# A spectral filter gated by a ReGLU network on one core: the second pair of row tiles turned by a transposing DMA in place of TensorE

## The chip, the cores and the metric

The kernel runs on one core of a Trainium2 chip. The metric is the device time of one execution in microseconds (us), median of three runs.

## The reference

```python
def reference(A_x, A_w_r, A_w_i, B_x, B_W_gate, B_W_up, B_W_down):
    def _A_ref(x, w_r, w_i):
        X = jnp.fft.rfft2(x, axes=(-2, -1)) * (w_r + 1j * w_i)
        return jnp.fft.irfft2(X, s=(S, D), axes=(-2, -1))
    def _B_ref(x, W_gate, W_up, W_down):
        gate = jnp.einsum("bsd,df->bsf", x, W_gate)
        up = jnp.einsum("bsd,df->bsf", x, W_up)
        h = gate * (gate > 0) * up
        return jnp.einsum("bsf,fd->bsd", h, W_down)
    x = A_x
    xn = _layernorm(x, axis=-1)
    return x + _A_ref(xn, A_w_r, A_w_i) * _silu(_B_ref(xn, B_W_gate, B_W_up, B_W_down))
```

`x` is 1 x 2048 x 512, the filter 2048 x 257 (real and imaginary part), the gate and up weights 512 x 1376, the down weights 1376 x 512, all in 32 bits.

## The kernel before

**Tiles.** The 2048 rows are 16 row tiles of 128 (partitions) by 512. They are handled in pairs, `c` = 0 to 7, and two pairs make a block of four row tiles, on which the gate and up products work. So pairs 0 and 1, row tiles one to four, are block 0; its transposed input is `xT0`, with columns 0 and 1 from pair 0 and 2 and 3 from pair 1. The 11 column blocks of the gate and up weights (10 of 128, the last of 96) come in groups `[0], [1], [2], [3,4], [5,6], [7,8], [9,10]`; `raw<g>_0` is the gate part of group g as loaded (32 bits), `raw<g>_1` the up part, and `wgu<g>` its 16-bit form.

**Products in three.** Every large product is made of 16-bit matmuls. A factor is split into a 16-bit high part and a low part (the rounding error, again in 16 bits), and the three passes high x high, high x low and low x high are added up in PSUM. A gate or up product is named `gu<block>_<column block>_<0 gate, 1 up>`; for one of them four slices of the 512 times three passes make a dozen matmuls, in the order of the slices: weights high with input high, weights high with input low, weights low with input high (`product`, L858). So the third matmul of a dozen needs the weights' low half, and the second the input's.

**Scaling the weights.** Before the split a group is multiplied by a power of two. ACT squares the raw weights and sums along the row (`squares`, L609); TensorE sums over the partitions with a column of ones (the `small<-m,ones` and `sum<-m,ones` matmuls); DVE makes the power of two from it (`csc`, three short steps, in some groups a fourth, `ups`; `group_scale`, L623); then the high half is written by ACT or DVE (`wgu<-raw,csc`) and the low half by DVE (SCALAR_TENSOR_TENSOR `wgu<-raw,csc,wgu`; `group_split`, L641).

**The start.** Row tiles are loaded by SP's queue, normalised (`stats`, `deviation`, `normalise`, L363 to L422: DVE statistics, ACT's square root, DVE's scaling to `xf<c>`), and turned, since a matmul takes the 512 along the partitions. Pair 0 is turned on TensorE in 32 bits, and its gate and up products with groups 0 and 1 run as fp32 matmuls straight from the raw weights (`gu<-xTf,raw`), so that TensorE has work while the weights are scaled. Pair 1 is turned on TensorE as well (`turn_row`, L496: eight fp32 transposes into PSUM, tile `head1`; then a cast for the high half and a subtraction for the low half, both out of PSUM). Pairs 2 to 7 go another way (`turn`, L438): ACT copies `xf<c>` to 16 bits (`x16_<c>`, high half), DVE or POOL subtracts for the low half, and SP issues one transposing DMA into `xT`, for pairs below 4 straight from SBUF (`DIRECT`, L61).

From there the A path (the two-dimensional transform as matmuls, stages y, xx, z, v, s) and the B path (gate, up, rectified product, down) are interleaved on TensorE.

**What sets the order.** Nothing is scheduled on the chip: each engine works its own list of instructions in order, with semaphores between engines, and SP issues nearly all DMAs, likewise in order. The lists come from a plan (`Plan`, L186). The code describes steps with what they read and write (`step`, L206); `run` (L233) emits them by the table `ORDER`; `PLACE` gives for each step that has a choice (`either`, L225) the engine, D for DVE, P for POOL, A for ACT; `SLOTS` gives the buffer of each tile. `folds` (`fold`, L530) make the even and odd parts of a pair's rows for the A path (`eo`, `ee`, `xs`).

Where the choice for pair 1 stands:

```python
if TURN1 == "PE":                       # L1291
    turn_row(1, 0)
    turn_row(1, 1)
...
            if k > 1 or k and TURN1 == "SP":     # L1300
                turn(k, LOWS[k])
```

Of the kernel before, what the change touches and what calls it, by code (L numbers as in the profile page):

```python
# [43 lines left out]
NORM, TURN1 = (('DVE', 'DVE'), ('DVE', 'DVE')), 'PE'  # L44
# [24 lines left out]
    4, 5, 6, 7, 8, 9, 10, 11, 12, 13, 14, 15, 16, 17, 32, 34, 33, 35, 36, 38, 37, 40, 39, 41, 143, 18, 19, 20, 21, 22, 23, 24, 25, 26, 27, 28, 51, 50,  # L69
    29, 30, 31, 144, 53, 42, 68, 52, 56, 57, 145, 146, 60, 61, 43, 45, 44, 46, 90, 89, 54, 147, 69, 92, 47, 48, 55, 480, 481, 91, 482, 483, 49, 70,  # L70
    79, 64, 99, 71, 93, 94, 100, 484, 58, 65, 97, 455, 62, 137, 120, 490, 140, 141, 138, 486, 487, 80, 66, 63, 485, 142, 139, 59, 492, 67, 119, 72,
    110, 73, 74, 95, 102, 101, 1235, 488, 489, 96, 109, 103, 410, 82, 77, 75, 98, 516, 104, 491, 493, 81, 107, 159, 76, 83, 105, 518, 456, 106, 122,
    149, 78, 112, 496, 124, 121, 123, 125, 528, 126, 408, 517, 148, 108, 175, 129, 494, 111, 113, 114, 150, 176, 177, 519, 529, 115, 178, 510, 182, 0,
    530, 497, 465, 151, 152, 522, 409, 629, 116, 131, 133, 511, 179, 628, 183, 117, 84, 407, 135, 136, 495, 626, 184, 185, 627, 413, 180, 181, 645,
    130, 118, 186, 520, 411, 127, 644, 132, 412, 414, 187, 512, 128, 134, 523, 1581, 87, 630, 466, 153, 154, 156, 467, 155, 631, 531, 158, 188, 524,
    189, 85, 161, 191, 415, 416, 554, 86, 192, 193, 219, 190, 632, 642, 220, 217, 525, 417, 157, 499, 513, 88, 546, 218, 160, 643, 633, 638, 162, 163,
    221, 498, 500, 418, 419, 420, 165, 1205, 526, 194, 501, 521, 552, 196, 646, 421, 197, 504, 195, 547, 164, 647, 422, 423, 222, 548, 502, 424, 648,
    534, 198, 505, 425, 634, 532, 649, 635, 166, 234, 426, 427, 553, 650, 654, 469, 167, 549, 640, 555, 223, 506, 507, 636, 508, 527, 453, 540, 428,
    651, 793, 168, 199, 536, 541, 791, 429, 225, 514, 430, 454, 431, 652, 224, 639, 584, 515, 255, 230, 271, 535, 252, 432, 612, 597, 231, 655, 433,
    556, 611, 503, 585, 434, 509, 637, 226, 542, 1, 656, 435, 436, 641, 598, 599, 610, 272, 537, 273, 437, 438, 256, 274, 227, 571, 572, 439, 600,  # L80
# [12 lines left out]
    780, 833, 354, 396, 339, 340, 767, 398, 399, 400, 470, 804, 805, 806, 834, 835, 836, 784, 787, 807, 808, 809, 810, 783, 785, 250, 355, 356, 837,
    786, 799, 800, 1171, 811, 801, 812, 464, 294, 357, 358, 359, 361, 341, 342, 324, 344, 477, 295, 343, 297, 296, 360, 402, 299, 298, 300, 328, 362,
    301, 401, 404, 363, 346, 1172, 302, 303, 788, 349, 403, 364, 304, 366, 838, 365, 368, 1206, 406, 802, 813, 306, 305, 839, 840, 814, 817, 843, 570,
    377, 367, 345, 369, 370, 1173, 347, 815, 307, 308, 841, 845, 844, 310, 847, 848, 846, 818, 348, 378, 381, 471, 472, 309, 850, 851, 380, 379, 382,
    385, 849, 386, 852, 1207, 854, 853, 857, 405, 1204, 473, 474, 855, 862, 1234, 864, 856, 860, 863, 350, 1169, 861, 865, 866, 867, 475, 858, 859,
    1208, 1209, 387, 869, 1174, 373, 374, 1210, 1238, 1239, 371, 372, 868, 383, 1240, 870, 871, 872, 1184, 803, 873, 1175, 1176, 1211, 876, 1177, 874,
    1178, 1212, 1213, 1236, 1237, 879, 1214, 875, 880, 881, 883, 1216, 1577, 1215, 1217, 882, 1179, 1181, 885, 1218, 1219, 1221, 884, 583, 886, 1220,
    888, 1180, 819, 1185, 1223, 889, 1186, 1222, 1182, 1241, 1187, 1224, 1225, 890, 891, 892, 893, 877, 1183, 887, 1226, 820, 1188, 1227, 1245, 902,  # L100
    904, 894, 1565, 1189, 903, 1242, 375, 895, 1190, 821, 351, 905, 1228, 1191, 1193, 1243, 1192, 1194, 376, 1246, 1244, 906, 909, 1229, 1230, 898,
    1195, 822, 907, 910, 1248, 896, 1231, 897, 1196, 913, 1247, 1249, 1250, 352, 1197, 823, 1232, 908, 911, 914, 923, 1198, 1199, 1200, 824, 825, 899,
    1233, 912, 826, 827, 1252, 915, 917, 816, 1561, 1253, 924, 878, 925, 1251, 927, 928, 1264, 1265, 1268, 1201, 1266, 1254, 918, 926, 930, 931, 1269,
    1270, 1202, 1255, 1256, 1203, 916, 828, 948, 900, 1267, 609, 1257, 1295, 934, 1275, 1276, 932, 933, 1258, 1271, 929, 1272, 919, 1277, 1274, 1273,
# [1360 lines left out]
```

## Time and profile before

| | |
|---|---|
| median of 3 runs | 388.42 us (387.67 to 388.53) |
| the profiled execution | 388.55 us |
| its span, first to last instruction | 386.8 us |
| mean granted TensorE clock | 1.000 |
| TensorE matmuls | 378.9 us busy, 98% of the span |
| VectorE (DVE) | 307.8 us, 80% |
| ScalarE (ACT) | 252.0 us, 65% |
| GpSimd (POOL) | 85.3 us, 22% |
| bytes moved by DMA | 77.95 MB, mean 202 GB/s |

In the profile PE is TensorE's matmuls, PEld its weight loads, which run beside matmuls, and SPq the DMAs issued by SP. All recorded instructions carry one line (L169, a helper), so they are told apart by the names of their tiles: `out<-in`, with the number of a block or group left out. An instruction row gives its start in us, its length, the engine, the instruction with tiles and shape, how many stand in the row, and in brackets the idle time before it with what ended it. Where several follow one another without a gap, the distance from start to start is less than the length, since an instruction's end overlaps the next one's beginning.

### The profile page before, as it was taken

Reading aid. Unit: us, or ns where it says so; the run is one execution under the profiler, and the core shown is the slowest. Engines: PE = TensorE matmul, PEld = TensorE weight load, DVE = VectorE, ACT = ScalarE, POOL = GpSimd, SP = SyncE. Lnnn points to the kernel's source line nnn. Section 1 sums busy time; section 2 is a strip of 40 time slices with the busy share of each in tenths; the row PEclk is TensorE's granted clock in tenths of the full one; section 3 lists DMA queues with packets and bytes.
Section 4 is the critical chain, followed back from the end, with each engine's and each line's share of the span. In section 5 each row is a group of like instructions: output and inputs, shape, how many; then the busy total and the mean of one; then the engine's idle time right before and its main releaser. Section 6 shows DMA issues by size and latency. Waiting matters only on the chain.

```text
span 386.8 us, 8906 instructions
## 1 busy us (share of the span) xinstructions
PE 378.9 (98%) x3525; PEld 261.3 (68%) x3525; DVE 307.8 (80%) x557; ACT 252.0 (65%) x490; POOL 85.3 (22%) x79
## 2 busy tenths in 40 slices
PE   8899999999999999999999999999999999999995
PEld 6755545445778777646888877755587787877544
DVE  6899999999678997994669882559377874399996
ACT  4899998999985565645476554764647662476411
POOL 2200203000232303001422087051105020214330
PEclk9999999999999999999999999999999999999999
DMA  7989878897579659878645647553652054999997
GB/s 259 407 288 305 245 134 255 274 259 199 186 188 289 191 174 289 272 146 236 198 158 185 146 114 217 164 143 90 205 130 78 2 162 117 232 212 248 223 254 188
DMA packets 67834, 77.95 MB, mean 202 GB/s; under 512 B 29073, under 2 KB 40945, under 8 KB 67793
## 3 DMA queue, kind: packets, MB, share of 16 engines
q1 hardware_dynamic: 66352, 74.77, 66.7%
q0 software_dynamic: 1440, 2.62, 4.3%
q8 instruction: 27, 0.44, 0.5%
q14 instruction: 15, 0.11, 0.1%
HBM read 46.95 MB, written 26.76 MB: 191 GB/s over the span
## 4 chain that ended last, share of the span: by engine, by line
PE 93%; DMA 2%; DVE 2%; ACT 1%; issue 0%; POOL 0%; SPq 0%; ACTq 0%
PE dn L169 28%; PE gu L169 17%; PE sb L169 15%; PE sa L169 10%; PE sc L169 10%; PE s L169 3%; PE z L169 3%; PE xx L169 3%; PE y L169 2%; DMA raw<-in_wu 2%; PE v L169 2%; DMA x<-in_x 1%; DVE t L169 1%; ACT wgu L169 1%; DVE xt L169 1%; DVE sv L169 0%
## 5 line engine op out<-in xcount | busy, mean ns | idle before, releaser
L169 PE MATMUL dn<-wds,h 128*128 128x512 f16 (+2 forms) x528 | 118.9, 372 | 0.0
L169 PEld LDWEIGHTS <-wgu 128*128 128x128 f16 x960 | 92.6, 98 | 37.7 <-issue 2.2
L169 PEld LDWEIGHTS <-h 128*128 128x128 f16 (+1 forms) x594 | 54.3, 98 | 51.4 <-issue 2.1
L169 PEld LDWEIGHTS <-wT 128*128 128x128 f16 x540 | 52.4, 98 | 9.3 <-issue 0.6
L169 PE MATMUL gu<-xT,wgu 128*128 128x512 f16 (+1 forms) x240 | 47.8, 358 | 0.0
L169 PE MATMUL sa<-xT,wgu 128*128 128x256 f16 x360 | 44.2, 273 | 0.0
L169 PE MATMUL sb<-xS,wT 128*128 128x256 f16 x360 | 44.2, 273 | 0.0
L169 PE MATMUL sc<-xS,wgu 128*128 128x256 f16 x180 | 22.1, 273 | 0.0
L169 PE MATMUL sc<-xT,wT 128*128 128x256 f16 x180 | 22.1, 273 | 0.0
L169 PE MATMUL sb<-xS,wgu 128*128 128x256 f16 x180 | 22.1, 273 | 0.0
L169 DVE TENSOR_TENSOR sc<-sb,sk 128x512 f32<-128x512 f32 x15 | 10.5, 698 | 12.7 <-PE sb L169 11.5
L169 ACT ACTIVATE sb<-sa 128x512 f32<-128x512 f32 x15 | 8.8, 585 | 13.7 <-PE sa L169 13.2
L169 DVE TENSOR_TENSOR t<-v,t 128x1024 f16<-128x1024 f32 x8 | 9.8, 1222 | 9.5 <-ACT t L169 9.4
L169 DVE TENSOR_TENSOR sr<-sb,sr 128x512 f32<-128x512 f32 x15 | 10.3, 686 | 8.6 <-PE sb L169 5.4
L169 PE MATMUL gu<-xT,wgt 128*64 128x256 f16 (+1 forms) x144 | 17.0, 309 | 0.0
L169 ACT ACTIVATE sq<-sc 128x512 f32<-128x512 f32 x15 | 8.9, 594 | 11.3 <-PE sc L169 7.9
L169 POOL TENSOR_TENSOR x<-xf,x 128x512 f16<-128x512 f32 x5 | 5.6, 1118 | 48.1 <-PE sb L169 38.8
L169 ACT ACTIVATE g<-dn,cdi 128x512 f32<-128x512 f32 (+1 forms) x16 | 10.5, 672 | 7.6 <-PE dn L169 7.5
L169 ACT ACTIVATE h<-se 128x512 f16<-128x512 f32 x15 | 9.4, 627 | 8.7 <-DVE se L169 6.0
L169 DVE TENSOR_TENSOR z<-z,z 128x1024 f16<-128x1024 f32 x8 | 9.8, 1223 | 6.6 <-ACT z L169 6.6
L169 ACT ACTIVATE t<-v 128x1024 f16<-128x1024 f32 x8 | 8.2, 1023 | 10.0 <-PE v L169 9.9
L169 ACT ACTIVATE p<-pf 128x1024 f16<-128x1024 f32 x8 | 8.5, 1057 | 9.4 <-DVE pf L169 7.7
(217 smaller groups left out, 740.8 us busy)
## 6 DMA issues: line engine op xcount, KB each, us to landing
rw<-in_wl SPq DMA_DIRECT2D x8, 512.0 KB, 4.2
A_d<-t SPq DMA_DIRECT2D x16, 256.0 KB, 3.7
wt<-in_wl SPq DMA_DIRECT2D x8, 512.0 KB, 4.3
at<-A_d SPq DMA_DIRECT2D x8, 512.0 KB, 4.6
C_d<-t SPq DMA_DIRECT2D x16, 256.0 KB, 3.2
ct<-C_d SPq DMA_DIRECT2D x16, 256.0 KB, 5.6
xf<-in_x SPq DMA_DIRECT2D x6, 512.0 KB, 5.0
N_d<-xf SPq DMA_DIRECT2D x6, 512.0 KB, 3.5
```

What stands on the lines that cost most here:

```text
L169: return lambda *args, **kw: self.tc.keep_in_program_order(f(*args, **kw))
```

## The change

Pair 1 (row tiles three and four) is turned as pairs 2 and 3 are. The eight fp32 transposes on TensorE, the two casts and the two subtractions from PSUM are gone. In their place ACT makes two copies to 16 bits, DVE two subtractions, and SP one transposing DMA of 128 x 16 x 128 from `x16_1` in SBUF to columns 2 and 3 of `xT0`. The three tables that set order, engines and buffers are new as a whole; the code is otherwise the same.

```diff
-NORM, TURN1 = (('DVE', 'DVE'), ('DVE', 'DVE')), 'PE'
+NORM, TURN1 = (("DVE", "DVE"), ("DVE", "DVE")), "SP"
...
 ORDER = (
-    4, 5, 6, 7, 8, 9, 10, 11, 12, 13, 14, 15, 16, 17, 32, 34, 33, 35, 36, 38, 37, 40, 39, 41, 143, 18, 19, 20, 21, 22, 23, 24, 25, 26, 27, 28, 51, 50,
...
+    4, 5, 6, 32, 34, 7, 8, 9, 10, 11, 12, 13, 33, 35, 14, 15, 16, 17, 18, 36, 19, 20, 21, 22, 23, 24, 25, 26, 27, 38, 37, 40, 467, 28, 39, 42, 29, 51,
```

The numbers behind a tile's name in the rows below are those of its buffer and version; `x4` counts instructions of one form.

TensorE, from the first fp32 products (`gu<-xTf,raw`) to the first 16-bit product of pair 1 (`gu0_0_0<-xT0,wgu0`). Before:

```order
MATMUL small_149<-m0_204,ones_127 128x2
MATMUL gu0_0_0_255<-xTf0_216,raw0_0_197 128x128 x4
MATMUL gu0_0_0_255<-xTf1_226,raw0_0_197 128x128 x4
MATMUL gu0_0_1_265<-xTf0_216,raw0_1_195 128x128 x4
MATMUL gu0_0_1_265<-xTf1_226,raw0_1_195 128x128 x4
LDWEIGHTS ones_127
MATMUL sum3_284<-m3_246,ones_127 128x2
MATMUL gu0_1_291<-xTf0_216,raw1_0_208 128x128 x4
MATMUL head1_303<-unit_101,xf1_249 128x128 x8
MATMUL gu0_1_291<-xTf0_216,raw1_1_275 128x128 x4
MATMUL gu0_1_291<-xTf1_226,raw1_1_275 128x128 x4
MATMUL gu0_1_291<-xTf1_226,raw1_0_208 128x128 x4
```

The same place in the changed kernel:

```order
MATMUL gu0_0_1_258<-xTf0_230,raw0_1_197 128x128 x4
LDWEIGHTS ones_127
MATMUL small_149<-m0_199,ones_127 128x2
MATMUL gu0_1_270<-xTf0_230,raw1_1_255 128x128 x4
MATMUL gu0_0_1_258<-xTf1_237,raw0_1_197 128x128 x4
LDWEIGHTS ones_127
MATMUL small_149<-m1_242,ones_127 128x2
LDWEIGHTS ones_127
MATMUL sum3_299<-m3_287,ones_127 128x2
MATMUL gu0_1_270<-xTf1_237,raw1_1_255 128x128 x4
MATMUL gu0_1_270<-xTf0_230,raw1_0_224 128x128 x4
MATMUL sum4_333<-m4_294,ones_127 128x2
```

The transposes `head1` are gone, the sums of groups 0 and 1 (`small`) come between the fp32 products, and the sum of group 4 (`sum4`), which came later before, stands ahead of the last of them.

VectorE, before, from the scaling of group 3's up weights to the low half of group 3's gate (`wgu3_105<-raw3_0`), which the third matmul of `gu0_4_0`, the gate dozen of column block 4, reads:

```order
TENSOR_SCALAR wgu3_105<-raw3_1_238,csc_122 128x1024
CAST xT0_296<-head1_303 128x512 x2
TENSOR_TENSOR xT0_296<-head1_303,xT0_296 128x512 x2
SCALAR_TENSOR_TENSOR h32_0_0_337<-gu0_0_1_265,ups_134,r0_0_310 128x256
SCALAR_TENSOR_TENSOR wgu0_102<-raw0_1_195,csc_122,wgu0_102 128x512
TENSOR_SCALAR csc_122<-small_149 128x2
TENSOR_SCALAR csc_122<-csc_122 128x2 x2
TENSOR_SCALAR ups_134<-csc_122 128x1
SCALAR_TENSOR_TENSOR wgu3_105<-raw3_0_240,csc_122,wgu3_105 128x1024
```

The same place in the changed kernel, after the two subtractions into `x16_1` and the `csc` steps and folds behind them:

```order
SCALAR_TENSOR_TENSOR wgu1_103<-raw1_0_224,csc_122,wgu1_103 128x512
TENSOR_TENSOR ee0_313<-eo0_227 128x4x129
TENSOR_SCALAR wgu0_102<-raw0_0_201,csc_122 128x512
TENSOR_SCALAR csc_122<-sum4_333 128x2x2
TENSOR_SCALAR csc_122<-csc_122 128x2x2 x2
SCALAR_TENSOR_TENSOR wgu0_102<-raw0_0_201,csc_122,wgu0_102 128x512
SCALAR_TENSOR_TENSOR wgu3_105<-raw3_1_264,csc_122,wgu3_105 128x1024
SCALAR_TENSOR_TENSOR wgu0_102<-raw0_1_197,csc_122,wgu0_102 128x512
TENSOR_TENSOR xT0_240<-xTf0_230,xT0_240 128x512
SCALAR_TENSOR_TENSOR wgu4_106<-raw4_0_268,csc_122,wgu4_106 128x1024
TENSOR_TENSOR xT0_240<-xTf1_237,xT0_240 128x512
SCALAR_TENSOR_TENSOR wgu3_105<-raw3_0_266,csc_122,wgu3_105 128x1024
```

Between the two subtractions and these rows stand `csc` and `ups` of group 1, a high half of group 1, the fold `xs0` of 516, and the `csc` steps of groups 3 and 0; between the last three rows a high half of group 1 (128 x 512). The low half of group 3's gate is row 42 of DVE's list in the changed kernel, and 37 in the one before; ahead of it now stand the two folds of pair 0 (`xs0`, which stood ahead of the scaling of `xf1`, and `ee0`, which was POOL's), the low halves of pair 0's `xT0` (both POOL's before), and the low half of group 4's gate.

SP's queue, from the load of pair 1's rows on. Before:

```order
DMA x1_206<-in_x 128x1024
DMA raw3_1_238<-in_wu 128x1024
DMA raw3_0_240<-in_wg 128x1024
DMA raw1_0_208<-in_wg 128x512
DMA raw1_1_275<-in_wu 128x512
DMA raw2_0_277<-in_wg 128x512
DMA raw4_0_280<-in_wg 128x1024
DMA raw4_1_289<-in_wu 128x1024
```

The changed kernel:

```order
DMA x1_194<-in_x 128x1024
DMA raw1_0_224<-in_wg 128x512
DMA raw1_1_255<-in_wu 128x512
DMA raw3_1_264<-in_wu 128x1024
DMA raw3_0_266<-in_wg 128x1024
DMA raw4_0_268<-in_wg 128x1024
DMA raw4_1_284<-in_wu 128x1024
DMA_TRANSPOSE xT0_240<-x16_1_279 128x16x128
DMA raw6_1_305<-in_wu 128x896
DMA raw6_0_320<-in_wg 128x896
DMA raw5_1_326<-in_wu 128x1024
```

Group 1 is now loaded ahead of group 3, group 2 later, and the transposing DMA stands between the loads of groups 4 and 6; it waits for DVE's subtractions, and everything behind it on SP with it.

More of the change, by code (lines that the diff above doesn't have):

```diff
@@ L68 @@
 ORDER = (
[59 rows of a table removed]
[59 rows of a table added]
 )
 PLACE = (
-    "AAPAAPAADDADADDDDDADDDDDDPDDDDADDDDDPPDAADAADDDPDPDDDPDPDPDDDDADPDDDDPADDAADDDAAAADDADDDDDDDPDPDDPDDADDDDDDDDPPDDDDDPDPPPDDDDPPPPDDDPDDDDDDD"
-    "DDDDDDDPDDDDDDDDDPDDDDDDDDDDDDDPDDDPPDDDPPDDPPDDPDPDDDDPPDDDDDPDDDDDDDDDDDPPDPPPPPPPDDPPDPDDDDPDDDDDDDPDPDDPPPPDDDDDDDDDDDDDDPDDDDDDDDDDDDDD"
-    "DDDDPDDDDDDDDDDDDDDDDDDDDDDDDDDDDDDDDDDDDDDDDDDDDDDDD"
+    "AADAADDADDADAAADDDDDAPPDDDDDDDADDDDDDPDDDAAAPDDDDPPPDDDDDDDDDDDDDPDDPDDDDADAADADADPDADDDDDPDDDDDDDDDDDDDDDDDDDADDDDDDDDDDDDDDDDDDDDPPDDDDDDD"
+    "DDDDDDDPDDDDDDPDDDDDDDDPDDDDDDDDPPDPPDPDPPDDPPDPPPDPPDPPDDPDDDPDDDPDDDDDDDDDDDDPDDDDPDDDPPDDDPDDDDDPPPDDDDDDDDDDDDDDDDDDDDDDDPDDDDDDDDDDDDPD"
+    "DDDDDDDDDDDDDDDDDDDDDDDDDDDDDDDDDDDDDDDDDDDDDDDDDDDDD"
 )
 SLOTS = (
-    "00003971325300000162115301630342017108930087200786590063006772923391298359131923024857316422006601103093382164681861322031291823095169091102"
-    "120114614263426102142040804066101551001a060292427725003142512311206340407051061124092612103201062103123a520103027902102310132012102421368513"
-    "04220213021a002132101702132306401200302531201012281319305051621012031a0211231650121301200021132034012130298007751704030212140808631406180129"
-    "20051745071517010211095034171525210200663709141918041172031812060705010945030726201307781412031619121610581119708741808037001161614659316520"
-    "215425413752009668300334122514671026"
+    "00003981321300000172132423221641157318901760319556080142005662310831050884135403139265316175704092213448392460090091018740284776083128177111"
+    "666535063644027102050031925167170181700a252342302520031101432506204760224071007837141870212130800212102750212032a100122322342013213281239310"
+    "012402101327a0210132320210320050012012041012023089075661402052103210372013032a02101021840210120351201123096071270302052103010303645703150110"
+    "15041417570801222012127987101414160108097008150203051621971319222400087173071816121509161003140004181205960110600339914194701645218302300423"
+    "511261806054717680354051075432626014"
 )
```

116 rows, old and new, of the table ORDER are left out of this document.

## The prediction

> **What bounds the kernel now.** I read the page's busy times first, then the chain that ended last, then busy time by stretches, and last the timeline of the first 25 us, since all that the change names happens there.
>
> ```profile
> PE 378.9 (98%) x3525; PEld 261.3 (68%) x3525; DVE 307.8 (80%) x557; ACT 252.0 (65%) x490; POOL 85.3 (22%) x79
> PE 93%; DMA 2%; DVE 2%; ACT 1%; issue 0%; POOL 0%; SPq 0%; ACTq 0%
> ```
>
> TensorE is busy for 98% of the span and carries 93% of the chain. The next view cuts the span into stretches: after the stretch come length, busy time (and instructions) of PE, PEld, DVE, ACT and POOL, then the granted clock, the DMA share and GB/s.
>
> ```profile
> 0.00:20.00 20.00, 16.56 (x130) 14.49 (x131) 14.91 (x44) 13.29 (x28) 4.40 (x11) 1.00 0.89 333
> 20.00:100.00 80.00, 80.00 (x478) 40.09 (x476) 75.58 (x151) 75.95 (x174) 6.40 (x5) 1.00 0.86 246
> 100.00:200.00 100.00, 99.91 (x971) 74.35 (x968) 80.42 (x146) 62.09 (x107) 24.57 (x21) 1.00 0.74 213
> 300.00:352.00 52.00, 52.00 (x597) 41.27 (x595) 36.38 (x57) 29.93 (x57) 7.34 (x8) 1.00 0.63 151
> ```
>
> From 20 us on PE never stops. So a microsecond lost or won before 20 us is a microsecond of the whole, unless later work stops PE, and only in the first 20 us (3.4 us idle) is there anything to win. The timeline of PE there (start, length, instruction, count, and the idle time before with what ended it):
>
> ```profile
> 13.38 0.16 PE L169 MATMUL sum<-m,ones 128*128 128x2 bf16 x1 [1.66 <-ACT wgu L169]
> 14.44 1.04 PE L169 MATMUL head<-unit,xf 128*128 128x128 f32 x8
> 15.32 2.84 PE L169 MATMUL gu<-xTf,raw 128*128 128x128 f32 x24
> 18.02 2.78 PE L169 MATMUL gu<-xT,wgu 128*128 128x256 f16 x24
> 20.67 2.75 PE L169 MATMUL gu<-xT,wgu 128*128 128x512 f16 x12
> 21.06 1.87 PEld L169 LDWEIGHTS <-wgu 128*128 128x128 f16 x10 [0.29 <-DVE wgu L169]
> 23.29 4.06 PE L169 MATMUL gu<-xT,wgu 128*128 128x512 f16 x24
> ```
>
> The `head` row is what the change removes: the second pair's eight transposes, 14.44 to 15.32, about 0.88 us of PE. After the fp32 products of the first pair (24 until 18.0) come the 16-bit products of the second pair, of the gate and up of column block 0 (18.02), then column block 4's gate (20.67), whose third matmul has to wait for the low half of its weights (PEld row, 21.06). From there to 23.29 is 2.23 us.
>
> **The change part by part.** *Removed:* 0.88 us of PE, and on DVE two casts and two subtracts out of PSUM.
>
> ```profile
> 14.26 0.75 DVE L169 SCALAR_TENSOR_TENSOR wgu<-raw,csc,wgu 128x512 f16<-128x512 f32 x1
> 14.93 0.75 DVE L169 TENSOR_SCALAR wgu<-raw,csc 128x1024 f16<-128x1024 f32 x1
> 15.60 1.28 DVE L169 CAST xT<-head 128x512 f16<-128x512 f32 x2
> 16.79 1.28 DVE L169 TENSOR_TENSOR xT<-head,xT 128x512 f16<-128x512 f32 x2
> 19.72 1.28 DVE L169 SCALAR_TENSOR_TENSOR wgu<-raw,csc,wgu 128x1024 f16<-128x1024 f32 x1
> 20.92 0.87 DVE L169 TENSOR_SCALAR wgu<-raw,csc 128x512 f16<-128x512 f32 x2
> 21.72 1.28 DVE L169 SCALAR_TENSOR_TENSOR wgu<-raw,csc,wgu 128x1024 f16<-128x1024 f32 x1
> 13.78 0.16 DVE L169 TENSOR_SCALAR csc<-sum 128x4 f32<-128x4 f32 x1
> 13.97 0.38 DVE L169 TENSOR_SCALAR csc<-csc 128x4 int32<-128x4 int32 x2
> 13.26 0.15 DVE L169 TENSOR_SCALAR ups<-csc 128x1 f32<-128x1 f32 x1
> 50.63 0.69 DVE L169 TENSOR_TENSOR ee<-eo 128x516 f32<-128x516 f32 x1
> 51.23 0.69 DVE L169 TENSOR_TENSOR xs<-eo 128x516 f32<-128x516 f32 x1
> ```
>
> In a row without gaps the prices are the distances from start to start: 0.67 for a SCALAR_TENSOR_TENSOR of 512 (14.26 to 14.93), 1.20 for one of 1024 (19.72 to 20.92), 0.40 for a TENSOR_SCALAR of 512 (20.92 to 21.72, two), 0.60 for a TENSOR_TENSOR of 512 or 516 (50.63 to 51.23; from PSUM the same, 15.60 to 16.79 for two), 0.48 for a chain of three `csc` steps (13.78 to 14.26), 0.19 for the `ups` behind a chain (an estimate from its 0.15). So DVE sheds 4 x 0.60 = 2.4 us.
>
> *Added, the source of the transposing DMA.* The second pair's halves must now stand in SBUF before SP may start.
>
> ```profile
> 8.61 0.69 DVE L169 BATCH_NORM_STATS2 st<-x 128x6 f32<-128x512 f32 x1 [0.29 <-DMA x<-in_x]
> 10.55 0.17 DVE L169 RECIPROCAL q<-q 128x2 f32<-128x2 f32 x1
> 11.98 0.19 ACT L169 ACTIVATE q<-q 128x2 f32<-128x2 f32 x1
> 12.20 0.55 DVE L169 TENSOR_SCALAR xf<-x,mv,q 128x512 f32<-128x512 f32 x1 [0.89 <-ACT q L169]
> 13.88 0.61 ACT L169 ACTIVATE wgu<-raw 128x512 f16<-128x512 f32 x1
> 52.28 1.13 ACT L169 ACTIVATE x<-xf 128x512 f16<-128x512 f32 x2
> 53.93 1.28 DVE L169 TENSOR_TENSOR x<-xf,x 128x512 f16<-128x512 f32 x2
> ```
>
> The statistics are over at 10.72. The square root on ACT came at 11.98 because ACT was at a square; in the new order a shorter square stands before it, so I put it at 10.75, `xf1` at 11.0 to 12.0 (two of about 0.5), ACT's square of the up weights (0.61) ahead of the copies, the two copies at 11.6 to 12.7 (1.13, as at 52.28), and the two subtracts behind them until **13.4** (as 53.93, where the last ends 1.8 after the copies' end; here the first starts after the first copy, so 0.7 after). Then SP issues.
>
> *Its landing* is read from the later transposes of the same size and form:
>
> ```profile
> 49.50 1.72 SPq L169 DMA_TRANSPOSE xT<-x  x1
> GB/s 348 341 301 246 212 164 143 96 55 14 0 0 0 0 0 0 0 0 0 0 0 0 0 0 102 232 280 294 290 287 287 290 280 266 492 273 273 229 75 10
> GB/s 0 0 0 0 0 0 0 7 7 7 10 10 10 7 10 10 10 58 276 283 290 300 280 294 300 280 294 294 302 376 437 382 382 83 0 0 0 0 0 0
> ```
>
> The two fine lines are slices of 0.075 us from 49 and from 52. The transfer issued at 49.50 moves its data in two bursts, up to about 54.5: 5.0 us. So `xT0` of the second pair is whole at T = 13.5 + 5.0 = **18.5**, where PE used to begin on it at 18.02. Bounds: 4.6 us (where the last of the full slices begin) gives 18.1; the slowest of the row-sum transposes, out of DRAM, gives 21.2:
>
> ```profile
> L169 SPq DMA_TRANSPOSE xS<-S_d x6: 1716/2921/4304, 80.8 to 257.0; - x6
> ...
> DMA to landing us min/median/max: 6.0/6.9/7.7
> ```
>
> The Trainium skill ("VectorE: DVE Perf Modes", "The three transpose paths") gives 390 ns for a 128x128 16-bit transpose on TensorE and 1309 ns by DMA; as an estimate from that page sixteen tiles one after another would take 21 us, land at 34.4 and put the total near 404. The bursts above speak against it: this trace's sixteen tiles took 5.0 us.
>
> *Moved, and this is the term that decides.* DVE works strictly in its order. From the subtracts' end (13.4) to the low half of block 4's gate (`wgu3<-raw3_0`, its row 42) the new order, as quoted with the change and filled in between, has 3 SCALAR_TENSOR_TENSOR of 1024 (3.60), 3 of 512 (2.01), 3 TENSOR_SCALAR of 512 (1.20), 2 TENSOR_TENSOR of 512 (1.20), 2 of 516 (1.20), 4 `csc` chains (1.92), 2 `ups` (0.38): 11.5 us, so it ends at 24.9 plus a tail of 0.1 = **25.0**. Before, that half (the row at 19.72) was ready at 21.00. What went in ahead of it: the two folds of 516, the lows of the first pair (on POOL before), a low half of group 4, and the halves that now start later since DVE first serves the transpose.
>
> PE meets this in order: block 0 gate from 18.5, where its third matmul waits for a low half that DVE ends at about 19.2, block 0 up (third matmul about 21.0), block 1's dozen (1.31, half of 24 in 2.65) until about 23.4, then block 4's gate, whose third matmul now waits until 25.1 in place of 23.9. It ends 2.23 later, at 27.3. Before, the same set, block 1's dozen included, is done at 23.29 + 1.31 = 24.60. The difference is **+2.7 us**; the 0.88 of the transposes and the 1.66 in front of `sum` are already in it, since PE's waits in the new order swallow both. After it PE has the same products to do and no idle time to take back. The other edits are covered: folds and lows exchanged between POOL and DVE are counted above; the loads queued on SP behind the transpose (groups 5, 6 and 2) are wanted by ACT only from 23 us on. If that cover fails, each microsecond of a late load is one of ACT's squares, not at once one of PE.
>
> **The rivals.** *(a) The transfer decides.* With T past 20.7 (25.1 less three dozens and two matmuls, 4.4) PE waits for xT0 longer than for DVE; at 21.2 that is +3.2, and with the loads behind it late as well up to +5.7. For: it shares the engines with 0.89 of load traffic in that stretch, and the row-sum transposes took up to 7.7. Against: 5.0 in the nearest row. 392.1 to 394.3. *(b) PE loses its pace in the new gaps.*
>
> ```profile
> L169 PE MATMUL small<-ones x28: 272/421/421, 1.2 to 5.9; 128*128 128x256 bf16 x28
> ```
>
> At the start the same matmul takes 421 ns and later 272; gaps of some 3 us between fp32 products and the halves could bring that back: one to two dozens at 1.5 times their time, +0.7 to +1.3, 392.0 to 392.6. Against: the granted clock is 1.00 in every stretch, and the gap of 1.66 slowed nothing. The Trainium skill ("TensorE: Matmul & The Clock Gate", Part 1) has a window of about 3.4 us of idling after which the clock halves; gaps under it cost nothing by that rule, and no run here shows the threshold. *(c) Not slower.* The lows are ready when PE asks: DVE would have to do the 11.5 us in about 9.9, by starting its weight halves in the waits before 13.4. Then T alone sets it: three dozens and block 4's 2.6 from 18.5 make 25.0, +0.4, and from 18.1, or with the fp32 work done at 17.6, 0 to -0.5: 388.0 to 389.0. For: the transposes are gone from PE and 2.4 us from DVE. Against: each of the rows before row 42 stands in DVE's order by name. *(d) Faster elsewhere:* the tail after 352, or the gap of 0.09 in 100 to 200; nothing in the first 20 us can give more than its 3.4 idle plus 0.88, and (c) keeps most of that out. 386 to 387.6.
>
> **How the numbers follow.** The sum is made against the profiled execution, 388.55 us (0.13 over the median 388.42): 388.55 + 2.7 = 391.3. Chances: the DVE term as worked out (390.5 to 392.0) 0.50; (a) 0.20; (b) 0.10; (c) 0.14; (d) 0.06. About 0.2% (0.8 us) is what a measurement of this kernel can tell from no change: of (c) 0.12 falls within it and 0.02 below, so faster 0.08, same 0.12, slower 0.80. The range takes in the forecast, (b), and (a) up to 394.3, and down to 389.0 where (c) begins.
>
> **What would show it.** Right: a PE wait of about a microsecond or more on DVE `wgu` near 23 to 25 us, gaps before 18.5 on ACT squares and the DMA, `sum4` on PE near 17, and 100% PE from 25.1 on. T wrong: the first `gu<-xT,wgu` starts away from 18.5. The forecast falls if DVE reaches the half of block 4 before 24, if PE idles anywhere after 28, or if block 4's gate ends before 25.5.

## The result and the profile after

| | before | changed |
|---|---|---|
| median | 388.34 us (4 runs, 387.67 to 388.53) | 392.15 us (4 runs, 391.56 to 393.45) |
| ratio to before | | 1.0104, 95% interval 1.0083 to 1.0125 |
| profiled execution | 388.55 us | 393.45 us |
| its span | 386.8 us | 391.7 us |
| granted TensorE clock of the four executions | | 0.99, 0.996, 1.00, 1.00 (393.45, 392.6, 391.7, 391.56 us) |

The changed kernel is about 1% slower, 3.8 us in the medians. The profiled execution is its slowest one. First the page of the changed kernel (busy times, and the engines' shares of the chain that ended last):

```profile
PE 381.3 (97%) x3517; PEld 263.2 (67%) x3517; DVE 315.0 (80%) x574; ACT 254.6 (65%) x489; POOL 63.5 (16%) x63
PE 93%; DVE 3%; DMA 2%; ACT 1%; issue 0%; POOL 0%; DVEq 0%
```

DVE has 7 us more and POOL 22 us less, mostly in stages where it doesn't matter; 3% of the chain is DVE's now. Busy time by stretches (columns as before; the third from the end is the granted clock):

```profile
0.00:20.00 20.00, 15.09 (x98) 13.25 (x99) 12.23 (x40) 13.81 (x31) 3.54 (x10) 0.88 0.81 255
20.00:30.00 10.00, 9.33 (x62) 6.54 (x61) 9.93 (x15) 9.28 (x20) 0.00 (x0) 0.90 0.90 336
30.00:60.00 30.00, 30.00 (x185) 14.88 (x183) 27.33 (x62) 27.64 (x67) 2.44 (x2) 1.00 0.90 274
100.00:200.00 100.00, 100.00 (x870) 73.06 (x869) 87.08 (x161) 62.91 (x111) 12.18 (x12) 1.00 0.70 200
```

Nearly all that differs lies ahead of 30 us: PE idles 4.9 us in the first 20 (3.4 before) and 0.7 in the next 10 (none before), and its clock is 0.88 and 0.90 there. The timeline of PE in that stage, with the kernel's last products:

```profile
11.09 2.03 PE L169 MATMUL gu<-xTf,raw 128*128 128x128 f32 x16
15.83 0.16 PE L169 MATMUL sum<-m,ones 128*128 128x2 bf16 x1 [2.70 <-ACT wgu L169]
15.85 3.76 PE L169 MATMUL gu<-xTf,raw 128*128 128x128 f32 x16
21.33 4.83 PE L169 MATMUL gu<-xT,wgu 128*128 128x256 f16 x38
26.82 2.33 PE L169 MATMUL gu<-xT,wgu 128*128 128x512 f16 x10 [0.67 <-DVE wgu L169]
28.99 0.17 PE L169 MATMUL sum<-m,ones 128*128 128x4 bf16 x1
385.74 1.17 PE L169 MATMUL dn_3b<-wds,h 128*128 128x128 f16 x18
```

And the same last row of the kernel before:

```profile
381.23 1.17 PE L169 MATMUL dn_3b<-wds,h 128*128 128x128 f16 x18
```

Four things are to be seen. The sum of group 3 waits 2.70 us for ACT. The 16 fp32 matmuls behind that gap take 3.76 us where 16 of the same form ahead of it took 2.03. Column block 4's gate waits for DVE's low half (0.67) and ends at 28.99; before, the same set was done at 24.60, so 4.4 us are lost by there. From there to the end of the last product it is 357.9 us (28.99 to 386.91) against 357.8 before (24.60 to 382.40): nothing is given back or lost later, but for 0.4 us in the tail behind the last product.

The clock by single microseconds, changed kernel:

```profile
14.00:15.00 1.00, 0.00 (x0) 0.00 (x0) 0.91 (x4) 1.00 (x3) 0.00 (x0) 1.00 0.47 193
16.00:17.00 1.00, 1.00 (x5) 1.00 (x6) 0.86 (x7) 1.00 (x3) 0.00 (x0) 0.50 1.14 212
20.00:21.00 1.00, 1.00 (x7) 1.00 (x6) 0.97 (x4) 1.00 (x2) 0.00 (x0) 0.50 0.97 387
22.00:23.00 1.00, 1.00 (x11) 0.89 (x10) 1.00 (x3) 1.00 (x4) 0.00 (x0) 1.00 0.99 368
```

It falls to half in the gap and stays there until just before 22 us. And the stations of the second pair's rows on DVE, ACT and SP:

```profile
9.58 0.69 DVE L169 BATCH_NORM_STATS2 st<-x 128x6 f32<-128x512 f32 x1 [2.57 <-DMA x<-in_x]
12.54 1.15 ACT L169 ACTIVATE x<-xf 128x512 f16<-128x512 f32 x2
13.21 1.29 DVE L169 TENSOR_TENSOR x<-xf,x 128x512 f16<-128x512 f32 x2 [0.24 <-ACT x L169]
14.53 1.97 SPq L169 DMA_TRANSPOSE xT<-x  x1
19.69 0.17 DVE L169 TENSOR_SCALAR csc<-sum 128x4 f32<-128x4 f32 x1 [0.69 <-PE sum L169]
25.48 1.28 DVE L169 SCALAR_TENSOR_TENSOR wgu<-raw,csc,wgu 128x1024 f16<-128x1024 f32 x1
```

The rows of pair 1 are there at 9.58 (8.61 before); DVE's stream to the low half of group 3's gate begins at 14.42 and ends at 26.76, with one wait of 0.69 in it, for the sum of group 4, which PE, at half pace, brings late. PE asks for that half at 26.16 (21.33 + 4.83), so it waits for it only the last 0.67 us.

### The profile page after: what moved, and what is told of

The parts are those of the page before. It is cut to its first block, busy times and chain, and to the rows that moved or that the text cites. A ratio compares the mean times of both kernels' runs of the same rounds, so it can differ in the third digit from the quotient of the medians.

```text
span 391.7 us, 8889 instructions
## 1 busy us (share of the span) xinstructions
PE 381.3 (97%) x3517; PEld 263.2 (67%) x3517; DVE 315.0 (80%) x574; ACT 254.6 (65%) x489; POOL 63.5 (16%) x63
## 3 DMA queue, kind: packets, MB, share of 16 engines
HBM read 46.95 MB, written 26.76 MB: 188 GB/s over the span
## 4 chain that ended last, share of the span: by engine, by line
PE 93%; DVE 3%; DMA 2%; ACT 1%; issue 0%; POOL 0%; DVEq 0%
PE dn L169 28%; PE gu L169 16%; PE sb L169 15%; PE sc L169 10%; PE sa L169 10%; PE s L169 3%; PE z L169 3%; PE xx L169 3%; DMA x<-in_x 2%; PE y L169 2%; PE v L169 2%; DVE wgu L169 1%; ACT wgu L169 1%; PE dn_3bb L169 0%; DVE st L169 0%; DVE xT L169 0%
## 5 line engine op out<-in xcount | busy, mean ns | idle before, releaser
L169 POOL TENSOR_TENSOR h<-sr,h 128x512 f16<-128x512 f32 x8 | 9.7, 1223 | 52.9 <-ACT h L169 52.9
L169 ACT ACTIVATE z<-z 128x1024 f16<-128x1024 f32 x8 | 8.2, 1024 | 13.7 <-PE z L169 13.7
L169 DVE TENSOR_TENSOR se<-sb,sk 128x512 f32<-128x512 f32 x15 | 10.3, 689 | 8.3 <-PE sb L169 7.4
L169 POOL TENSOR_TENSOR h<-se,h 128x512 f16<-128x512 f32 x8 | 9.5, 1187 | 43.8 <-ACT h L169 43.8
L169 POOL TENSOR_TENSOR x<-xf,x 128x512 f16<-128x512 f32 x2 | 2.3, 1160 | 83.0 <-ACT x L169 43.4
L169 DVE TENSOR_TENSOR a<-y,a 128x1024 f16<-128x1024 f32 x8 | 9.7, 1222 | 6.1 <-ACT a L169 6.0
L169 ACT ACTIVATE sk<-sc 128x512 f32<-128x512 f32 x15 | 8.9, 595 | 8.7 <-PE sc L169 8.2
```

The lines of the kernel that those rows point to most:

```text
L169: return lambda *args, **kw: self.tc.keep_in_program_order(f(*args, **kw))
```

## The experiments

The theories: **O**, the new order of DVE and ACT makes a weight half late for TensorE, as predicted; **C**, the halved ("cold") clock behind the gap; **L**, the loads' order, which lets pair 1's rows land later; **T**, the transposing DMA itself, by its landing. Each kernel was run in several rounds beside the kernel before; ratios are to that. In the diffs `put(a, b, c)` moves steps b and c in the changed kernel's `ORDER` to right behind step a:

```python
def put(after, *steps):
    rest = [s for s in ORDER if s not in steps]
    k = rest.index(after) + 1
    return (*rest[:k], *steps, *rest[k:])
```

**1. Idle matmuls in the gap** (`e1_warm`), in front of the sum of group 3:

```diff
+        def total():
+            for k in range(24 * (g == 3)):
+                matmul(T["small"][:, 256:], ones[:, 0:P], ones, start=True, stop=True)
             matmul(to()[:, :2 * nf], ones[:, :P], T[f"m{g}"][:, :2 * nf], start=True, stop=True)
```

> The changed kernel with 24 idle matmuls (128x256, some 2.6 us) on TensorE ahead of the sum of group 3, in the gap from 13.0 to 15.8 us; nothing else. Theory C (the gap takes the TensorE clock down, and the fp32 products behind it then run at half pace): the granted clock is 1.00 throughout, the 16 fp32 matmuls behind the gap take 2.0 us in place of 3.8, the wait of DVE for the sum of group 4 (0.69) goes, and the time is 391.2 to 391.7, with a spread of the executions under 0.5 us in place of 1.9. Theory O alone (only the late low half on DVE counts, the clock doesn't): 392.0 to 393.5 as before.

393.04 us (392.95 to 393.45), ratio 1.0123 (1.0109 to 1.0136). The clock stayed at 1.00 and the spread fell to 0.5 us, but the time didn't fall. PE in that kernel:

```profile
14.00 2.78 PE L169 MATMUL small<-ones 128*128 128x256 bf16 x24 [1.48 <-DVE csc L169]
16.62 0.17 PE L169 MATMUL sum<-m,ones 128*128 128x2 bf16 x1
26.79 2.33 PE L169 MATMUL gu<-xT,wgu 128*128 128x512 f16 x10 [0.82 <-DVE wgu L169]
```

The idle matmuls write the PSUM tile `small`, which DVE was still to read, so they began only at 14.00 and pushed the sum of group 3 to 16.62. That spoils the test of C. PE waits for DVE's half at 26.8 although the clock is at 1.00, but DVE itself stood 1.29 us waiting for that late sum, so the run doesn't speak for O either.

**2. The lows in TensorE's order** (`e2_lows`): on ACT and DVE, group 3's gate first.

```diff
+ORDER = put(102, 95, 66, 62, 97, 489)
+ORDER = put(104, 105, 65, 67, 59, 63, 96, 98, 106, 77)
```

Here 95, 97 and 105 are ACT's high halves of group 3's gate and up and of group 4's gate, 96, 98 and 106 their low halves on DVE, 65, 66 and 67 those of group 0, 59, 62 and 63 pair 0's part of `xT0`, 489 ACT's reading of column block 0's first products.

> The changed kernel with ACT's and DVE's steps between the scale of group 4 and the first gate product of column block 4 in the order in which TensorE asks for them: the low half of group 3's gate ahead of those of group 3's up and group 4's gate. Theory O (the DVE order sets the end of this stage): that half is ready at 24 us in place of 26.8, TensorE's wait of 0.67 there goes, and the time falls by 0.7 to 1.3, to 390.9 to 391.5. Theory T (the transfer or the cold fp32 products bind anyway, the half is only near the end): under 0.4 us of change, 391.8 to 392.3.

392.21 us (391.84 to 393.33), ratio 1.0096 (1.0081 to 1.0112): no change. The wait at column block 4 went, and another came:

```profile
15.88 0.16 PE L179 MATMUL sum<-m,ones 128*128 128x2 bf16 x1 [2.85 <-ACT wgu L179]
21.53 8.21 PE L179 MATMUL gu<-xT,wgu 128*128 128x256 f16 x48 [2.40 <-ACT r L179]
```

Step 489 reads the PSUM tile into which the next products go; put behind ACT's high halves, it ended at 21.47 and is what PE waited for last. Most of the 2.40 us would have been lost without it: the transposing DMA, issued at 14.58, landed 6.3 us later, at 20.9. The clock fell in that gap. So this order traded one wait for another and decides nothing.

**3. The load of in_sp back** (`e3_s4`):

```diff
+ORDER = put(466, 467)
```

> The changed kernel with the load of in_sp (128x16, pieces of 64 bytes) back from SP's third place to behind the load of the edge weights. Theory L (its small pieces slow the loads behind it, the second pair's rows land 1 us late, and this opens the gap ahead of the sum of group 3 from under 2 to 2.7 us): the statistics of pair 1 begin at 8.6 in place of 9.6, the gap is under 2 us, the clock stays at 1.00, the transposing DMA is issued at 13.5, and the time is 390.3 to 391.0. If the small load doesn't matter (other loads queued close behind pair 1's rows share its bandwidth): statistics at 9.4 or later and 391.6 to 392.5.

391.33 us (390.83 to 393.18), ratio 1.0083 (1.0065 to 1.0101): 0.8 us less in the median, the intervals overlap, and the time lies between the two forecasts. The statistics began at 8.64, yet L is not shown by that: experiment 11, with this load early, had them at 8.41. The landing of pair 1's rows differs from one profiled execution to the next (8.2 to 9.6 over all of these kernels; with the loads in the changed kernel's order 8.4 to 9.6). PE in this execution:

```profile
14.88 0.16 PE L178 MATMUL sum<-m,ones 128*128 128x2 bf16 x1 [2.36 <-ACT wgu L178]
14.90 3.56 PE L178 MATMUL gu<-xTf,raw 128*128 128x128 f32 x16
25.67 2.33 PE L178 MATMUL gu<-xT,wgu 128*128 128x512 f16 x10 [0.82 <-DVE wgu L178]
```

Pair 1 a microsecond earlier, and DVE's half, PE's wait for it and the end of column block 4 (27.84) are 1.1 us earlier too. The clock fell all the same, behind a gap of 2.36.

**4. All three** (`e6_all`): the edits of 1 to 3 together.

> The three edits together. If order, clock and load are the whole loss and the transfer itself costs nothing: 388.0 to 388.9, as before the change. If the transfer's landing (6.1 us behind its issue at 13.5, so 19.6, where the kernel before began on the same tile at 18.0) is what remains: TensorE waits for xT0 until 19.6 and the time is 389.2 to 390.2. If theory O is wrong and something later in the new order costs time: 391 or more.

392.70 us (392.36 to 393.57), ratio 1.0115 (1.0100 to 1.0131): it carries the faults of 1 and 2 (PE waits 1.2 us ahead of the idle matmuls, 1.5 for ACT's reading, and 1.2 for DVE's `h` at 31.8), and tells no theory apart, though by its number it lies in the last range (391 or more).

**5. Turned on TensorE, new order** (`e4_pe`): the three tables of the change, the transposes in the gap.

```diff
-NORM, TURN1 = (("DVE", "DVE"), ("DVE", "DVE")), "SP"
+NORM, TURN1 = (("DVE", "DVE"), ("DVE", "DVE")), "PE"
...
+TURNED = {153: (137, 140, 138), 154: (139,), 155: (141,), 156: (142,), 157: ()}
+ORDER = tuple(m for n in ORDER for m in TURNED.get(n, (n if n < 137 else n + 6 if n < 153 else n + 1,)))
```

> The changed kernel's three tables with pair 1 turned on TensorE again: the eight fp32 transposes stand where TensorE would otherwise wait for group 3's squares, ACT makes two casts and DVE two subtractions from PSUM in the places of the two copies and two subtractions for the DMA, so ACT and DVE have the same load. Theory O (the new order of ACT and DVE is the loss, not the transfer): the low half of group 3's gate is as late as in the changed kernel (25.5 to 26.5 us) and the time is 391.0 to 392.2; only the cold executions go, since the gap is 0.9 us shorter. Theory T (the transposing DMA, its landing and what queues behind it, is the loss): 388.3 to 389.5.

395.18 us (394.77 to 395.67), ratio 1.0175 (1.0153 to 1.0196), outside both forecasts.

```profile
17.77 0.16 PE L174 MATMUL sum<-m,ones 128*128 128x2 bf16 x1 [4.11 <-ACT wgu L174]
28.76 2.33 PE L174 MATMUL gu<-xT,wgu 128*128 128x512 f16 x10 [0.82 <-DVE wgu L174]
```

ACT stood 2.1 us until the transposes were done and 0.8 more between its two casts, ahead of group 3's squares, so the sum came 2 us later than in the changed kernel. It isn't the clean comparison that it was meant to be; it shows that here the delay on ACT ahead of those squares was paid in full: the sum, the end of column block 4 (30.93 against 28.99) and the profiled time are all 2 us later.

**6. Turned by SP, old order** (`e5_sp`): the tables of before, with the five steps of the new turn in the places of the old.

```diff
-NORM, TURN1 = (('DVE', 'DVE'), ('DVE', 'DVE')), 'PE'
+NORM, TURN1 = (('DVE', 'DVE'), ('DVE', 'DVE')), 'SP'
...
+TURNED = {49: (49, 153, 155), 94: (94, 154, 156), 120: (120, 157), 137: (), 138: (), 139: (), 140: (), 141: (), 142: ()}
+ORDER = tuple(m for n in ORDER for m in TURNED.get(n, (n if n < 137 else n - 6 if n < 159 else n - 1,)))
```

> The other half: the tables of before with pair 1 turned by SP's transposing DMA alone (ACT's copies behind xf1, DVE's subtractions behind the scale of group 3, the transfer behind the load of group 6's up weights, its source in a buffer that is free). Theory O: DVE has two operations less before the low half of group 3's gate, which is ready by 21; what is left is the landing, issue at about 15.5 and 5 to 6 us, T = 20.5 to 21.5 in place of 18.0, less 0.9 for the transposes' end at 17.1: TensorE waits 3.4 to 4.4 us and the time is 390.9 to 392.5, with a cold clock behind that gap in some executions. If the landing were no cost: 387.5 to 388.5.

394.51 us (393.30 to 394.83), ratio 1.0153 (1.0131 to 1.0175); outside both forecasts; the clock was 0.990 to 0.993 in the executions.

```profile
18.81 0.16 PE L174 MATMUL small<-m,ones 128*128 128x2 bf16 x1 [1.73 <-ACT wgu L174]
20.74 4.45 PE L174 MATMUL gu<-xT,wgu 128*128 128x256 f16 x24 [1.77 <-DMA xT<-x]
```

The DMA was issued at 15.74 and waited for until 20.74: 5.0 us, within the 5 to 6 that were expected. PE waits 1.73 us for ACT (which has two copies more) and 1.77 for the landing, and the 24 products behind run cold (4.45 against 2.78). So the turn alone, with its steps in these places, costs 6.2 us in the old order; the new tables win 2.4 of that back.

**7 and 8. A second try at the order, turned by SP and by TensorE** (`e7_sp_best`, `e8_pe_best`): in_sp's load back, the reading on ACT kept ahead, 9 idle matmuls ahead of the sum of group 1 (7 only).

```diff
+ORDER = put(466, 467)
+ORDER = put(102, 489, 95, 66, 62, 97)
+ORDER = put(104, 105, 65, 67, 59, 63, 96, 98, 106)
+ORDER = put(488, 499, 491, 492, 77)
```

> The changed kernel with the load of in_sp back, ACT's and DVE's steps in the order in which TensorE asks (the reading of the first products on ACT kept ahead this time, and the three steps on DVE that release PSUM put ahead of the up weights of group 4), and 9 idle matmuls ahead of the sum of group 1, where they wait for nothing. Theory O: the half of group 3's gate is ready at 23 to 23.5, the first 16-bit product starts when the transfer lands (19.6), column block 4's gate ends at 26.2 and the time is 389.6 to 390.4 with the clock at 1.00. If DVE's total work up to 32 us binds whatever its order: 390.8 or more, with the wait moved to a later tile.

> The same order edits and in_sp's load, without the idle matmuls, on the tables of the changed kernel with pair 1 turned on TensorE. Its difference to the kernel before it in this list is the price of the transposing DMA when both have the better order. Theory O: DVE sets both, and they lie within 0.6 us of each other, 389.2 to 390.2 here. Theory T: this one is faster by 1 us or more, 388.0 to 389.0.

394.61 us (393.15 to 395.83), ratio 1.0159 (1.0134 to 1.0184), and 397.29 us (396.33 to 397.62), ratio 1.0223 (1.0200 to 1.0247); theory O is met by neither, and the first is in the range of its rival (390.8 or more). Both lose to one row, here that of the first:

```profile
25.40 5.74 PE L181 MATMUL gu<-xT,wgu 128*128 128x256 f16 x24 [3.27 <-DVE h L181]
```

Step 499, DVE's reading of column block 1's PSUM tile, was written ahead of the products into the other half of that tile, so PE waited for it, behind all the low halves. The second has the late squares of experiment 5 besides (4.11 us again), so the difference of the two is no price of the DMA.

**9, 10, 11. The order, its fault mended** (`e9_all`: order, load and 9 idle matmuls; `e10_s4_warm`: load and idle matmuls only; `e11_order`: order only). The order edits:

```diff
+ORDER = put(103, 489, 95, 66)
+ORDER = put(484, 497, 62, 97, 105)
+ORDER = put(104, 65, 67)
+ORDER = put(488, 59, 63, 96, 98, 106, 495, 499, 491, 492, 77, 142, 78, 143, 107, 108)
```

> The kernel with all three edits once more, with one fault taken out: in the earlier version TensorE's products of column block 1 were made to wait for DVE's step that reads the same PSUM tile, because that step was written ahead of them; now it is written behind them, and ACT's reading of that tile stands early. Theory O (the order of DVE and ACT is the loss, the transfer itself costs little): the transfer lands at 18.4, the low half of group 3's gate is ready at 22.6, column block 4's gate has no wait and ends at 25.0 to 25.6 against 29.0 in the changed kernel and 24.6 before; the time is 388.7 to 389.6. If the total of DVE's work binds in any order: a wait at a later tile and 390.5 or more.

> The same without the order edits: only in_sp's load moved back and the 9 idle matmuls ahead of the sum of group 1. Theory O: the clock is 1.00 in every execution, DVE's half is ready at 25.4 to 25.7 as when the load alone was moved, TensorE waits for it, column block 4's gate ends at 27.6 to 27.9, and the time is 390.5 to 391.2 with a spread under 0.6 us. If load and clock were the whole loss: 388.5 to 389.5, like the kernel with all edits.

> The order edits alone on the changed kernel (in_sp's load early, no idle matmuls). Theory O: DVE's half is ready at about 24 where the sum of group 4 comes late and TensorE no longer waits for DVE; the fp32 products, cold in some executions, and the landing at 19.0 to 20.6 set the start of the 16-bit products, column block 4's gate ends at 26 to 28 and the time is 390.0 to 391.6. If order is not the loss: 391.6 to 393.0.

390.80 us (9 runs, 390.43 to 391.83), ratio 1.0061 (1.0041 to 1.0081); 391.57 us (391.15 to 392.46), ratio 1.0077 (1.0052 to 1.0103); 390.82 us (390.31 to 391.90), ratio 1.0065 (1.0040 to 1.0090). With all edits the interval is just clear of the changed kernel's: 1.3 us less. The order alone reaches the same median, but its interval overlaps; load and idle matmuls without it stand between. 9 and 10 differ by the order alone: 0.8 us, with intervals that overlap. The kernel of 9, DVE's three low halves of 1024 and PE:

```profile
21.35 3.67 DVE L182 SCALAR_TENSOR_TENSOR wgu<-raw,csc,wgu 128x1024 f16<-128x1024 f32 x3
...
15.27 0.16 PE L182 MATMUL sum<-m,ones 128*128 128x2 bf16 x1 [1.55 <-ACT wgu L182]
19.62 6.47 PE L182 MATMUL gu<-xT,wgu 128*128 128x256 f16 x46 [0.74 <-DVE wgu L182]
26.51 0.16 PE L182 MATMUL sum<-m,ones 128*128 128x4 bf16 x1 [0.41 <-ACT wgt L182]
```

The gate's half is the first of the three and ready at 22.6, as expected; column block 4 no longer waits and ends at 26.1. Yet the time missed theory O's 388.7 to 389.6 and lies in the range of its rival (390.5 or more). Three smaller waits are left: the sum of group 3 (15.27 against 13.38 before), 0.74 for group 0's low half, which DVE makes only behind the scale of group 4, and 0.41 for ACT's squares of group 6. In the profile of 10 PE waits for DVE at column block 4:

```profile
25.52 2.33 PE L178 MATMUL gu<-xT,wgu 128*128 128x512 f16 x10 [0.67 <-DVE wgu L178]
```

It ends that block at 27.68, as theory O had it, with the clock at 0.998 to 1.00 in every execution, and DVE's stream doesn't wait for PE there: this is the clearest sight of O without C. Time and spread (1.3 us) are above what was forecast. In the profile of 11 the landing came up:

```profile
19.57 8.35 PE L181 MATMUL gu<-xT,wgu 128*128 128x256 f16 x48 [1.41 <-DMA xT<-x]
```

Issued at 13.35, landed 6.1 us later, where in 9 it took 4.4.

**12. The landing taken away** (`e12_early`): on the kernel of 11.

```diff
+    early = wT[-1][:, 0:2]
+    POOL.memset(early, 0.0)
...
+            of = early.rearrange("p a b c d -> p (a b c d)") if c == 1 else x16().rearrange("p i h d -> p (i h d)") if DIRECT[c] else X_d[c]
+            SP.dma_start_transpose(xt.rearrange("p i k r -> p (i k) r"), of)
```

> The kernel with the order edits alone, with the transposing DMA reading another tile that is zeroed by GpSimd at the start, so that it waits for nothing and lands long before 18 us; ACT's copies and DVE's subtractions are still made. Columns 2 and 3 of xT0 hold zeros in place of pair 1's rows. It takes away the landing alone. If the landing (TensorE's wait of 1.4 us for it, and the cold clock behind that wait) is what is left of the loss besides ACT and DVE: the 16-bit products start at 18.1 to 18.5, the granted clock stays near 1.00, and the time falls from 390.8 to 389.2 to 390.2. If ACT's later squares and DVE's work set what is left: under 0.5 us of change, 390.4 to 391.2. If the landing is all of it: 388.2 to 388.9.

391.30 us (390.62 to 392.37), ratio 1.0083 (1.0063 to 1.0103): not faster than 11. Its profiled execution (390.62 us), the DMA's landing first:

```profile
7.05 8.22 SPq L181 DMA_TRANSPOSE xT<-wT  x1
...
DMA to landing us min/median/max: 11.8/11.8/11.8
...
18.96 6.68 PE L181 MATMUL gu<-xT,wgu 128*128 128x256 f16 x48 [1.01 <-ACT xf L181]
25.48 0.17 PE L181 MATMUL sum<-m,ones 128*128 128x4 bf16 x1
36.53 1.28 PE L181 MATMUL gu<-xT,wgt 128*64 128x256 f16 x20 [0.64 <-DVE wgt L181]
```

The landing was not taken away. Issued at 7.05 among the loads, the transfer held SP for 8.22 us and landed 11.8 us later, at 18.85, only 0.6 before that of 11; the first product starts right behind it (the row names ACT, whose `xf` gives PE nothing). The time is just above the forecasts' ranges. So the test of T failed, and how fast the new order would be with a free landing stays open. What it does show: column block 4 ends at 25.48, the earliest of these kernels, and 0.64 is lost again at 36.5, where DVE is late with another half: a wait at a later tile, as the rival in experiments 7 and 9 had it.

## Why the prediction held, and where its size was off

**The bound.** Right: nearly everything was decided ahead of 30 us, and a microsecond there is a microsecond of the whole (357.9 against 357.8 us from column block 4's end to the last product).

**The DVE term.** As a length it was right. From the subtractions' end to the low half of group 3's gate the sum had 11.5 us; measured are 14.42 to 26.76, 12.3, less the 0.69 of waiting: 11.6. PE waits for that half at column block 4, as said. In the profiles of experiments 3 and 10 the rows land earlier, the stream starts earlier and its end moves with it. But it binds by less than was forecast: PE waited 0.67, where the forecast had 1.2 (25.1 in place of 23.9). With the half in time, column block 4 would have ended at about 28.3 (an estimate: 26.16 + 2.17), still 3.7 behind the kernel before. Experiments 9, 11 and 12, with the half earlier in the stream, lose this wait, and 9 against 10 puts 0.8 us on the order. So the late half is what PE waits for last in this stage, as predicted, but it isn't shown to be the whole loss: ACT's squares, the landing and the half come within a microsecond or two of each other, and when one is taken away the next binds.

**Three terms were mis-sized.** The start of the stream: the forecast took the rows of pair 1 to land as before (8.61); in the profiled execution they came at 9.58. Since this landing differs as much between executions of other kernels, it isn't shown to belong to the change. Then DVE's wait of 0.69 for the sum of group 4, which wasn't in the sum. With both, 27.3 + 1.0 + 0.7 = 29.0, and column block 4 ended at 28.99. Third, T: it was put at 18.5 and came at 20.6, the issue at 14.53 in place of 13.5 and the landing 6.1 in place of 5.0. PE began on the tile at 21.33, later still, because its fp32 products ran at half pace. By the forecast's own sign (the first 16-bit product away from 18.5) T was wrong; the sum hid it, since DVE's half came last.

**The number.** The executions at a clock of 1.00 (391.7 and 391.56) are within 0.4 us of the forecast's 391.3 and in the band of the DVE term; the other two, 392.6 and 393.45, are above it. The median, 392.15, lies just above that band, where (a) and (b) were priced. How near it came depends on how many of four executions were cold, which is luck; and the two at 1.00 have no profile, so their terms aren't known one by one.

**Rival (b), the clock,** was priced as another way; its mechanism came together with the forecast's in half of the executions. It was priced at 1.5 times the matmuls' time; measured is 3.76 against 2.03. In the profiled one it is PE's half pace from 15.1 to 21.9 that makes the sum of group 4 late. For the same 48 products (column blocks 0, 1 and 4) the price is plain: 8.35 us in experiment 11 and 8.21 in 2, where the clock fell, against 6.68 in 12 and 4. What it costs in the time of the kernel is less settled: the two cold executions of the changed kernel were 0.9 to 1.9 us slower than the others, but among those of experiment 11 the clocks of 0.994 to 0.996 and of 1.00 spread over the same range, and experiment 10, always warm, is no faster than 3, always cold. In the profiles in which DVE is the last to be ready, cold products ahead of it cost only what DVE itself waits for (0.69 in the changed kernel).

**Rival (a), the transfer,** didn't decide the changed kernel. Its landing there:

```profile
DMA to landing us min/median/max: 6.1/6.1/6.1
```

That is 20.6, ahead of the last fp32 product (21.3) and early enough for DVE's half at 26.8 (20.6 + 4.4 = 25.0). In the other profiles where it was issued behind the subtractions it took 4.4 to 6.3 us, the forecast's bounds but for the shortest. It is the next bound, though: in experiments 6, 11 and 12 PE starts on the tile only as it lands, after 1.8, 1.4 and 1.0 us of waiting. The estimate of 21 us from the Trainium skill ("VectorE: DVE Perf Modes", "The three transpose paths") is far from all of these; even the transfer that was issued among the loads took 11.8.

**Rival (c)** needed the lows in time; even in experiment 9, where the half for column block 4 was, no execution came below 390.4, and no kernel here came to 389.0.

**What the change was worth.** The transposes' 0.88 us of TensorE and DVE's two operations less were not regained. On ACT the square root that waits for pair 1's rows, a square of group 1 and the two copies now stand ahead of both of group 3's squares, which TensorE waits for next; and DVE got a fold and the two lows that POOL had. That is read from the order in the traces; no run took the copies alone away. The best of these kernels, 390.80, is still above the kernel before. Of the 1.9 us by which its column block 4 and the sum behind it are late (26.51 against 24.60), 0.5 is the later end of the fp32 products, 0.74 and 0.41 are the two waits; a quarter of a microsecond is in no row. A turn on TensorE with its transposes well placed in the new order wasn't tried, so what the transposing DMA costs against TensorE's transposes in one and the same order stays open.

## What to carry to other kernels

When work is taken off the bounding engine, list what its replacement puts on the engines that feed it, in their order, up to the next tile that the bounding engine asks for: that list, priced by start-to-start distances, gave the length of DVE's stream here to 0.1 us (11.5 against 11.6). It didn't give the loss alone, because other paths ended close by: list those too. Three reorderings here (experiments 2, 4 and 7) moved a reader of a shared PSUM tile so that TensorE stood behind it; look for those before the order is changed. And a gap on TensorE is to be judged together with the idle time around it, since the clock may fall for the work behind it (3.76 us for 2.03 here).

## What was not expected of the hardware

The one transposing DMA that was issued among the queued loads was slow and held its queue: 8.22 us of SP and 11.8 to the landing in experiment 12, a single profile, against 2 to 3 us and 4.4 to 6.3 where it stood behind them.

The clock falls on less than a full stretch of idling, and stays low for fixed times. Slices of 0.2 us around the two edges, of the changed kernel, then of experiments 3, 11 and 2:

```profile
15.00:15.20 0.20, 0.00 (x0) 0.00 (x0) 0.18 (x2) 0.20 (x1) 0.00 (x0) 0.77 0.35 143
21.80:22.00 0.20, 0.20 (x3) 0.15 (x2) 0.20 (x1) 0.20 (x2) 0.00 (x0) 0.66 0.73 300
```

```profile
14.60:14.80 0.20, 0.00 (x0) 0.00 (x0) 0.20 (x2) 0.20 (x3) 0.00 (x0) 0.80 0.06 21
18.00:18.20 0.20, 0.20 (x4) 0.20 (x3) 0.04 (x1) 0.20 (x1) 0.00 (x0) 0.67 0.41 108
```

```profile
19.60:19.80 0.20, 0.20 (x3) 0.17 (x4) 0.20 (x2) 0.20 (x1) 0.00 (x0) 0.92 1.01 412
23.00:23.20 0.20, 0.20 (x3) 0.14 (x2) 0.20 (x1) 0.20 (x2) 0.00 (x0) 0.55 0.82 328
```

```profile
21.20:21.40 0.20, 0.00 (x0) 0.00 (x0) 0.20 (x2) 0.20 (x2) 0.00 (x0) 0.70 0.97 392
24.60:24.80 0.20, 0.20 (x3) 0.12 (x2) 0.20 (x1) 0.20 (x2) 0.00 (x0) 0.77 0.67 266
```

Where a slice's mean lies between 1.00 and 0.50 it gives the moment of the edge: low from 15.11 to 21.94 (6.83 us), from 14.72 to 18.13 (3.41), from 19.77 to 23.18 (3.41) and from 21.28 to 24.69 (3.41), one or two times the same 3.4 us. In experiment 11 the fall came behind gaps of 0.29 and 1.41 us with products between them: in the 3.4 us ahead of it PE idled 1.7. The Trainium skill ("TensorE: Matmul & The Clock Gate", Part 1) describes a free-running window of about 3.4 us, and the low times agree with that; that a whole window must be idle doesn't agree, here about half of one was enough. A gap of 1.66 in the kernel before left the clock alone. So did a longer one: experiment 2 idled for 2.85 us, from 13.03 to 15.88, at a clock of 1.00, where experiment 3 fell in a gap of 2.36. The length of a gap therefore doesn't decide alone. Counted back by 3.41 us from experiment 2's fall at 21.28, a boundary would lie at 14.46, in the middle of that gap, which fits stretches that run on by themselves; no run tests it.
